# Another order for the single operations of attention and the first product group

## The chip, the cores and the metric

The kernel runs on one core of one Trainium2 chip. The metric is the device time of one execution in microseconds; lower is better. Within a core the engines work side by side, each through its own list of instructions in a fixed order: TensorE (PE) multiplies, VectorE (DVE), ScalarE (ACT) and GpSimd (POOL) do elementwise work, and SyncE (SP) issues the transfers between HBM and the on-chip memory (SBUF). An instruction waits on semaphores for its inputs and for the place it writes to, and whatever stands behind it on the same engine waits with it.

## The reference, cut to what matters

```python
# q, k, v: (4 batches, 8 heads, 576 tokens, 64); attention inside chunks of 64 tokens
scores = scale * np.matmul(q_c, k_c.transpose(0, 1, 2, 4, 3))
scores = scores - np.max(scores, axis=-1, keepdims=True)
attn = np.exp(scores)
attn = attn / (np.sum(attn, axis=-1, keepdims=True) + 1e-09)
out = np.matmul(attn, v_c)
x = out as 2304 tokens x 512
x = (x @ w_a) * (x @ w_b) @ w_out          # w_a, w_b 512 x 1536, w_out 1536 x 512
h = x @ w_in                               # 512 x 2048
g = np.maximum(h, 0.0) + alpha * np.minimum(h, 0.0)
return g @ w_out2                          # 2048 x 512
```

## The kernel before

The 2304 tokens are 18 units of 128, handled in nine pairs (0 to 8). The first pair makes up token block 0, pairs 1 and 2 block 1, 3 and 4 block 2, 5 and 6 block 3, 7 and 8 block 4. For attention each unit loads its q and k (512 KB, three buffers) and its v (three small transfers). The weights of the first product group come in blocks of 512 KB as 64-bit words, through two buffers, and are put together as float32 by ScalarE, VectorE and GpSimd; each is then split into a high and a low half. Every matrix product is three products of halves, 12 matmuls for a tile of 128 rows and one block of tokens.

The program has two parts. From the second on (`after_attention`) a planner orders everything by costs and due times. The first part, attention and the first product group on blocks 0 to 3, follows the string `START` near the top of the file: 304 words, each one operation, performed in that order (`perform`). So `START` sets the order on every engine, and it also sets who gets the next buffer of a ring: there are four PSUM banks for products and transposes, two PSUM places for scores and attention outputs (tag `s`), three SBUF places shared by the transposed probabilities and the first product of a group (tag `a`), two for probabilities (tag `e`).

A word is letters and a number: a pair, a pair's unit behind `U` (pairs 0 and 1 are done by unit), or block and part behind a dot. `t` and `c` count units throughout, so `t10` is the first unit of pair 5. The chain of one pair is

- `Lk` load q and k (SP, L1691), `s` scores (PE, L1735), `m` maximum (DVE, L1741), `u` subtract it (DVE, L1745), `e` exponential (ACT, L1751), `z` sum and `r` reciprocal (DVE, L1755, L1759 and L1760), `n` normalise (POOL, L1764)
- `t` transpose (PE, L1771), `c` copy out (ACT, L1778), `Lw` load v (SP), `v` times v (PE, L1793), `h` high half of x (ACT, L1812), `l` low half of x (DVE, L1816)

and that of one weight block is `Lf` load (SP, L248), `o` (ACT, L258 and L259), `d` (DVE, L266, L267, L270), `a` (POOL, L280), `H` high half (ACT, L285), `V` or `W` low half (POOL or DVE, L290). `F` is one product of the first layer (`F1.3`: block 1, part 3; even parts are a, odd parts b), `E` takes it out of PSUM (ACT L395 for even parts, DVE L405 for odd ones, which multiplies b by a), `h1.1` and `g1.1` are the halves of that result (ACT L376, POOL L381), `B` one product of the second layer and `D` its way out (ACT L432). Waits that matter below: `u` of a pair writes where the pair two before it had its probabilities, so it comes after that pair's `t`; a score tile goes where an older score tile or attention output was read last; a transfer waits until the transfer eight before it has landed.

The function `keep_busy` puts 24 matmuls on zeros among the first scores (L1685), behind the words `sU0`, `sU2` and `t0`; it is in both versions.

Of the kernel before, what the change touches and what calls it, by code (L numbers as in the profile page):

```python
# [27 lines left out]


START = """  # L30
Lk0 Lf0 sU0 Lk1 mU0 uU0 o0 d0 Lk2 sU1 mU1 eU0 zU0 rU0 sU2 Lf1 o1 uU1 a0 nU0 Lk3 mU2 sU3 Lk4 d1 Lk5 a1 Lw0
Lf2 uU2 Lw1 eU1 mU3 uU3 H0 eU3 zU1 t0 s2 V0 eU2 Lk6 Lk7 rU1 nU1 c0 o2 zU3 t1 c1 H1 vU0 zU2 rU2 Lw2 vU1 nU2
hU0 rU3 m2 hU1 Lw3 t2 nU3 t3 c3 Lk8 c2 u2 lU0 s3 lU1 e2 F0.0 E0.0 vU2 V1 vU3 d2 z2 Lw4 a2 r2 H2 F0.1 Lf3 n2
o3 m3 t5 hU2 u3 E0.1 V2 hU3 Lk9 Lw5 d3 Lk10 s4 lU2 lU3 a3 Lk11 Lw6 e3 t4 F0.2 Lk12 c5 c4 H3 m4 v2 u4 V3 F0.3
Lf4 h0.1 g0.1 z3 h2 l2 e4 E0.2 s5 r3 z4 F1.0 r4 Lf5 n3 o4 E0.3 E1.0 Lk13 t6 m5 d4 F1.1 h0.3 Lk14 t7 n4 c6
F1.2 E1.1 g0.3 o5 a4 u5 d5 a5 c7 e5 Lw7 t9 H4 z5 h1.1 g1.1 t8 v3 s6 H5 Lf6 F1.3 Lw8 h3 c9 r5 V4 E1.2 Lw9
Lk15 m6 V5 n5 c8 l3 B0.0 Lw10 u6 v4 E1.3 t11 t10 s7 o6 D0.0 m7 h1.3 h4 c11 l4 g1.3 d6 e6 B0.1 z6 B1.0 B1.1
c10 Lw11 a6 D0.1 D1.0 r6 Lf7 B0.2 o7 u7 v5 D0.2 h5 n6 D1.1 B1.2 Lw12 B0.3 d7 e7 Lk16 D0.3 B1.3 t12 D1.2 F2.2
D1.3 z7 Lw13 r7 n7 t13 c12 l5 F2.0 F2.3 Lw14 c13 v6 E2.2 E2.3 E2.0 t15 F2.1 t14 h6 l6 E2.1 F3.0 Lw15 Lk17
h2.3 h2.1 g2.3 c15 s8 Lw16 g2.1 B2.0 m8 H6 a7 c14 D2.0 E3.0 v7 F3.1 B2.1 E3.1 u8 F3.2 B2.2 h3.1 F3.3 h7 l7  # L40
Lf8 e8 z8 H7 Lf9 D2.1 r8 E3.2 Lw17 n8 D2.2 E3.3 g3.1 V6 t17 t16 B2.3 c16 c17 h3.3 g3.3 v8 h8 l8 D2.3 W7
"""


# [1861 lines left out]
```

## Time and profile before

| | us |
|---|---|
| median of 3 runs (lowest, highest) | 846.9 (846.26, 846.99) |
| the profiled execution, its own time | 845.54 |
| its span, first to last instruction | 843.6 |
| PE busy in the span | 833.2 |
| DVE, ACT, POOL busy | 704.3, 434.5, 199.3 |
| mean granted TensorE clock (share of full speed) | 0.998 |

The work of `START` ends on PE at about 100 us of the span. A busy PE counts matmuls that overlap, so the step from one start to the next is the better measure of what an operation takes.

### The profile page before, as it was taken

The page shows a single profiled execution, that of the slowest core. Times are in us where ns is not written, and L with a number is a line of the kernel's source. Part 1 is how long each engine was busy: PE and PEld are TensorE (multiplying, and loading weights), DVE is VectorE, ACT ScalarE, POOL GpSimd, SP SyncE. Part 2 cuts the span into 40 slices and gives each one's busy share as a digit, 9 for nine tenths or more (in the row PEclk, how much of TensorE's full clock was granted, in tenths as well). Part 3 has the DMA queues.
Part 4 walks back from the last instruction along what each step waited for, and adds up shares of the span by engine and source line. Part 5 has one row for each costly group of instructions (what it writes and reads, how often), then busy time and mean ns, then how long its engine had stood idle before and what let it go on. Part 6 is the DMA issues. An engine that isn't in the chain of part 4 may idle for free.

```text
span 843.6 us, 15744 instructions
## 1 busy us (share of the span) xinstructions
PE 833.2 (99%) x5676; PEld 727.8 (86%) x5676; DVE 704.3 (83%) x1165; ACT 434.5 (52%) x762; POOL 199.3 (24%) x158
## 2 busy tenths in 40 slices
PE   7999999999999999999999999999999999999998
PEld 6888888888888888888888888989999899999998
DVE  6983388988888989898899999999889876677786
ACT  4673576554555445554456567654336435444441
POOL 4553234423342321421321233111103000000000
PEclk9999999999999999999999999999999999999999
DMA  8953367778658531899999699897657679665543
GB/s 317 301 182 112 101 200 219 226 252 271 224 164 311 175 113 50 262 333 386 341 349 334 228 320 363 290 339 214 213 185 222 194 237 293 214 187 171 181 150 125
DMA packets 137357, 197.14 MB, mean 234 GB/s; under 512 B 15424, under 2 KB 79424, under 8 KB 137280
## 3 DMA queue, kind: packets, MB, share of 16 engines
q1 hardware_dynamic: 137280, 196.15, 70.2%
q8 instruction: 45, 0.74, 0.4%
q14 instruction: 32, 0.26, 0.1%
HBM read 138.42 MB, written 57.67 MB: 232 GB/s over the span
## 4 chain that ended last, share of the span: by engine, by line
PE 97%; DMA 1%; DVE 1%; ACT 0%; issue 0%; SPq 0%; DVEq 0%
PE po L368 20%; PE pa L368 11%; PE pb L368 11%; PE l4X L1444 11%; PE sumX L1042 10%; PE pX L1042 6%; PE l4Z L1444 5%; PE sumZ L1042 5%; PE pZ L1042 3%; PE l4Y L1444 3%; PE ph L368 3%; PE sumY L1042 3%; PE pY L1042 2%; PE s L1793 1%; PE pt L1771 1%; PE s L1735 1%
## 5 line engine op out<-in xcount | busy, mean ns | idle before, releaser
L728 POOL TENSOR_TENSOR t<-t,raw 128x512 int32<-128x512 int32 x60 | 82.8, 1380 | 249.7 <-DVE t L720 119.9
L1171 DVE TENSOR_TENSOR acc<-po,acc 128x512 f32<-128x512 f32 (+1 forms) x100 | 63.0, 633 | 15.5 <-PE po L368 14.6
L1042 PE MATMUL sumX<-T,w 128*128 128x512 f32 x248 | 65.6, 392 | 0.0
L368 PE MATMUL po<-gh,wl 128*128 128x512 f32 (+1 forms) x176 | 64.0, 364 | 0.0
L368 PE MATMUL po<-gl,wh 128*128 128x512 f32 (+1 forms) x176 | 63.6, 361 | 0.0
L368 PE MATMUL po<-gh,wh 128*128 128x512 f32 (+1 forms) x176 | 63.4, 360 | 0.0
L1444 PE MATMUL l4X<-w,h 128*128 128x256 f32 x308 | 62.7, 283 | 0.0
L368 PE MATMUL pa<-xh,wl 128*128 128x512 f32 (+1 forms) x160 | 58.0, 363 | 0.4 <-DVE wl L757 0.4
L368 PE MATMUL pb<-xh,wl 128*128 128x512 f32 (+1 forms) x160 | 57.8, 362 | 0.0
L368 PE MATMUL pa<-xl,wh 128*128 128x512 f32 (+1 forms) x160 | 57.3, 358 | 0.0
L368 PE MATMUL pb<-xl,wh 128*128 128x512 f32 (+1 forms) x160 | 57.3, 358 | 0.0
L368 PE MATMUL pa<-xh,wh 128*128 128x512 f32 (+1 forms) x160 | 57.2, 358 | 0.0
L368 PE MATMUL pb<-xh,wh 128*128 128x512 f32 (+1 forms) x160 | 57.2, 357 | 0.0
L753 ACT ACTIVATE wh<-t 128x512 fp32r<-128x512 f32 x60 | 37.6, 627 | 30.9 <-POOL t L728 29.0
L1042 PEld LDWEIGHTS sumX<-T,w 128*128 128x128 f32 x248 | 44.7, 189 | 7.7
L1444 PEld LDWEIGHTS l4X<-w,h 128*128 128x128 f32 x308 | 49.4, 191 | 1.2
L697 ACT ACTIVATE t<-raw 128x512 f32<-128x512 f32 x60 | 39.8, 664 | 15.4 <-DMA raw<-in_moe_w_out 7.7
L757 DVE TENSOR_TENSOR wl<-t,wh 128x512 fp32r<-128x512 f32 x52 | 42.4, 821 | 2.1 <-ACT wh L753 2.1
L1444 PE MATMUL l4X<-w,l 128*128 128x256 f32 x156 | 44.0, 282 | 0.0
L720 DVE SCALAR_TENSOR_TENSOR t<-raw,t 128x512 uint32<-128x512 uint32 x60 | 42.2, 704 | 1.3
L368 PE MATMUL po<-gh,w 128*128 128x512 f32 x128 | 43.2, 389 | 0.0
L702 ACT ACTIVATE raw<-raw 128x512 int32<-128x512 uint32 x60 | 40.0, 667 | 2.1 <-DMA raw<-in_moe_w_out 2.1
(272 smaller groups left out, 2419.2 us busy)
## 6 DMA issues: line engine op xcount, KB each, us to landing
w<-dw SPq DMA_DIRECT2D x134, 256.0 KB, 4.1
w<-dw SPq DMA_DIRECT2D x194, 128.0 KB, 3.3
dw<-wl SPq DMA_DIRECT2D x62, 256.0 KB, 4.5
dw<-wh SPq DMA_DIRECT2D x61, 256.0 KB, 4.9
raw<-in_moe_w_out SPq DMA_DIRECT2D x28, 512.0 KB, 4.2
qk_t<-in_qkv SPq DMA_DIRECT2D x18, 512.0 KB, 5.3
raw<-in_moe_w_in SPq DMA_DIRECT2D x16, 512.0 KB, 4.5
raw<-in_moe_w_a SPq DMA_DIRECT2D x12, 512.0 KB, 4.1
```

The source lines that it names most:

```text
L368: nc.tensor.matmul(out=dst, lhsT=a, rhs=b, start=(i == 0), stop=(i == len(steps) - 1))
L697: nc.scalar.activation(out=x, in_=st["raw"][:, :, 1].bitcast(F32), func=ACTF.Abs)
L702: nc.scalar.activation(out=lo.bitcast(I32), in_=lo, func=ACTF.Copy, scale=2.0**-29)
L720: nc.vector.scalar_tensor_tensor(out=u, in0=st["raw"][:, :, 1], scalar=0xC0000000, in1=u, op0=ALU.bitwise_and, op1=ALU.bitwise_or,)
L728: nc.gpsimd.tensor_tensor(out=i, in0=i, in1=st["raw"][:, :, 0].bitcast(I32), op=ALU.add)
L753: nc.scalar.activation(out=st["h"], in_=F[key], func=ACTF.Copy)
L757: ENG[t.engine].tensor_tensor(out=l, in0=F[key], in1=st["h"].bitcast(F32), op=ALU.subtract)
L1042: nc.tensor.matmul(out=dst, lhsT=x, rhs=y, start=opens and kk == n == 0, stop=kk == 1 and n == 2, skip_group_check=not opens,)
L1171: nc.vector.tensor_tensor(out=a, in0=b, in1=a, op=ALU.add)
L1444: nc.tensor.matmul(out=dst[:, tt], lhsT=x, rhs=y, start=opens and tt == i == 0, stop=i == 5, skip_group_check=tt > 0 or not opens,)
L1735: nc.tensor.matmul(out=s[q, i, kk, hp % 2, hp // 2 ^ i, :], lhsT=t[r, 0, hp, q], rhs=t[r, 1, hp, q])
L1771: nc.tensor.transpose(out=pt[:, h, i, :], in_=e[:, i, u % U, h].rearrange("p o k -> p (o k)"), identity=ident)
```

## The change

The 304 words of `START` are put in another order; the words are the same, no other line changes, and every operation still comes after what it needs. A line of it:

```diff
 START = """
-Lk0 Lf0 sU0 Lk1 mU0 uU0 o0 d0 Lk2 sU1 mU1 eU0 zU0 rU0 sU2 Lf1 o1 uU1 a0 nU0 Lk3 mU2 sU3 Lk4 d1 Lk5 a1 Lw0
+Lk0 Lf0 Lk1 sU0 Lk2 Lf1 mU0 o0 uU0 eU0 d0 zU0 sU1 Lk3 mU1 rU0 sU2 Lk4 Lk5 uU1 a0 mU2 o1 d1 sU3 eU1 zU1 nU0
...
```

The second part of the program is the same instruction for instruction. On PE the order is the same up to `F0.1`; after it attention runs further ahead (`t4` before `s4`, pairs 3 to 8 earlier), and all eight products `B1` and `B2` stand at the end of the part. On SP `Lf2` stands behind `Lw1 Lw0 Lk6`, where it stood behind `Lw0` alone, and `Lk9 Lw5` stand ahead of `Lk8 Lw4`.

On VectorE, behind the conversion of the second weight block (rows L266 to L270), the unit chains of pairs 0 and 1 stood like this before (`mx`, `e` and `sm` with the numbers 207 and 239, 308 are pair 1; `e_139`, `sm_167` are the second unit of pair 0):

```order
L1745 TENSOR_TENSOR e_239<-s_171,mx_207 128x2x256
L1741 TENSOR_REDUCE mx_207<-s_171 128x2x4
L1745 TENSOR_TENSOR e_239<-s_171,mx_207 128x2x256
L1755 TENSOR_REDUCE sm_167<-e_139 128x2x4
L1759 TENSOR_SCALAR sm_167<-sm_167 128x2x4
L1760 RECIPROCAL sm_167<-sm_167 128x2x4
```

And now (`e_146`, `sm_152` are pair 0, `e_234`, `sm_294` pair 1):

```order
L1755 TENSOR_REDUCE sm_152<-e_146 128x2x4
L1745 TENSOR_TENSOR e_234<-s_175,mx_207 128x2x256
L1759 TENSOR_SCALAR sm_152<-sm_152 128x2x4
L1760 RECIPROCAL sm_152<-sm_152 128x2x4
L1741 TENSOR_REDUCE mx_207<-s_175 128x2x4
L1755 TENSOR_REDUCE sm_294<-e_234 128x2x4
L1759 TENSOR_SCALAR sm_294<-sm_294 128x2x4
L1760 RECIPROCAL sm_294<-sm_294 128x2x4
L1745 TENSOR_TENSOR e_234<-s_175,mx_207 128x2x256
```

The sum and reciprocal of pair 0's second unit (`zU1 rU1`) stand ahead of the last maximum and subtraction of pair 1 (`mU3 uU3`), not behind them.

On ScalarE, from the second transposed unit (`c1`, `ptt_t_315`) to the third and fourth, before:

```order
L258 ACTIVATE t_305<-raw_237 128x512
L259 ACTIVATE raw_237<-raw_237 128x512
L1778 ACTIVATE ptt_t_315<-pt_310 128x512
L285 ACTIVATE wh_317<-t_199 128x512
L1812 ACTIVATE xh0_360<-s_319 128x4x128 x2
L1778 ACTIVATE ptt_t_383<-pt_378 128x512
L1778 ACTIVATE ptt_t_387<-pt_372 128x512
L1751 ACTIVATE e_389<-e_389 128x1024
```

And now (`c1` is `ptt_t_327`):

```order
L1778 ACTIVATE ptt_t_327<-pt_304 128x512
L285 ACTIVATE wh_353<-t_209 128x512
L1812 ACTIVATE xh0_355<-s_309 128x4x128 x2
L258 ACTIVATE t_362<-raw_329 128x512
L259 ACTIVATE raw_329<-raw_329 128x512
L1778 ACTIVATE ptt_t_370<-pt_365 128x512
L1751 ACTIVATE e_381<-e_381 128x1024
L1778 ACTIVATE ptt_t_436<-pt_376 128x512
```

The third weight block (`o2`, L258 and L259) went from ahead of `c1` to ahead of `c2`.

Later, on GpSimd, the stretch that ends in the normalising of pair 5 (`n5`, the last L1764 row) was this before (`a4 a5 g1.1 V4 V5 n5`):

```order
L280 TENSOR_TENSOR t_726<-t_726,raw_658 128x512
L280 TENSOR_TENSOR t_785<-t_785,raw_723 128x512
L381 TENSOR_TENSOR gl_813<-a_sb_730,gh_811 128x512
L290 TENSOR_TENSOR wl_914<-t_726,wh_807 128x512
L290 TENSOR_TENSOR wl_926<-t_785,wh_886 128x512
L1764 TENSOR_TENSOR e_789<-e_789,sm_809 128x1024
```

And it is now (`a4 a5 V4 g0.3 g1.1 V5 n5`):

```order
L280 TENSOR_TENSOR t_721<-t_721,raw_632 128x512
L280 TENSOR_TENSOR t_839<-t_839,raw_802 128x512
L290 TENSOR_TENSOR wl_914<-t_721,wh_904 128x512
L381 TENSOR_TENSOR gl_916<-a_sb_704,gh_899 128x256
L381 TENSOR_TENSOR gl_961<-a_sb_837,gh_912 128x512
L290 TENSOR_TENSOR wl_965<-t_839,wh_906 128x512
L1764 TENSOR_TENSOR e_730<-e_730,sm_866 128x1024
```

`g0.3` (256 columns) moved in between `a5` and `n5`. What `a5` (the second row) waits for is `d5` on VectorE, which now stands behind the taking out of `F0.3` and `F1.1`:

```order
L405 TENSOR_TENSOR a_sb_704<-pb_789,a_sb_704 128x256
L405 TENSOR_TENSOR a_sb_837<-pb_708,a_sb_837 128x512
L266 TENSOR_SCALAR t_839<-t_839 128x512
L267 TENSOR_SCALAR t_839<-t_839 128x512
L270 SCALAR_TENSOR_TENSOR t_839<-raw_802,t_839 128x512
```

Before, `F0.3` was taken out well ahead of it (`E0.3 m5 d4 E1.1 u5 d5`), since on PE `F0.3` came before `F1.0`; now `F0.3` comes after `F1.1 F1.0 v3`, and PE goes on with `s6 t8 t9 F1.3 F1.2 v4 s7 t10 t11 F2.0`.

## Rows read from the trace of the kernel before

**Rows 1.** The page: busy time, share and count by engine
```profile
PE 833.2 (99%) x5676; PEld 727.8 (86%) x5676; DVE 704.3 (83%) x1165; ACT 434.5 (52%) x762; POOL 199.3 (24%) x158
```

**Rows 2.** Stretches: start:end, length, busy by engine (count), PEclk, DMA share, GB/s
```profile
90.00:100.00 10.00, 10.00 (x106) 8.26 (x107) 4.13 (x6) 5.75 (x10) 4.86 (x4) 1.00 0.19 50
...
19.00:19.50 0.50, 0.49 (x18) 0.49 (x21) 0.41 (x1) 0.47 (x1) 0.50 (x1) 0.50 0.98 391
```

**Rows 3.** Waits of PE, 0 to 160: total us, times, longest
```profile
PE pt L1771 <- POOL e L1764: 1.8, 2, 1.5
```

**Rows 4.** Timeline of PE: start, us, instruction, idle time before and releaser
```profile
15.03 0.69 PE L1735 MATMUL s<-qk_t 64*64 64x64 f32 x32 [0.81 <-DMA qk_t<-in_qkv]
17.19 0.66 PE L1771 MATMUL pt<-ident,e 128*128 128x128 f32 x4 [1.46 <-POOL e L1764]
...
20.07 1.97 PE L1771 MATMUL pt<-ident,e 128*128 128x128 f32 x8
...
23.20 0.39 PE L368 MATMUL pa<-xh,wl 128*128 128x256 f32 x1
...
27.99 0.66 PE L1771 MATMUL pt<-ident,e 128*128 128x128 f32 x4 [0.37 <-POOL e L1764]
```

**Rows 5.** Timeline of DVE, pair 1's subtraction and pair 0's sum
```profile
12.97 0.68 DVE L1745 TENSOR_TENSOR e<-s,mx 128x512 f32<-128x512 f32 x1
14.89 0.68 DVE L1755 TENSOR_REDUCE sm<-e 128x8 f32<-128x512 f32 x1
```

**Rows 6.** Timeline of POOL, normalising pair 0's second unit
```profile
16.09 1.04 POOL L1764 TENSOR_TENSOR e<-e,sm 128x512 f32<-128x512 f32 x1 [0.39 <-DVE sm L1760]
```

**Rows 7.** Timeline of SP and ACT: Lf2 issued, Lk6 and Lk7 issued, o2
```profile
11.56 0.59 SPq L248 DMA_DIRECT2D raw<-in_moe_w_a  x1
...
15.06 0.82 SPq L1691 DMA_DIRECT2D qk_t<-in_qkv  x2
...
17.22 0.68 ACT L258 ACTIVATE t<-raw 128x512 f32<-128x512 f32 x1 [0.58 <-DMA raw<-in_moe_w_a]
```

**Rows 8.** Tile qk_t, 0 to 40: its loads
```profile
DMA to landing us min/median/max: 3.7/5.4/6.6
```

**Rows 9.** Timeline of PE later: a first-layer product, then v4, t11 and t10
```profile
36.91 0.50 PE L368 MATMUL pa<-xh,wl 128*128 128x512 f32 x1
...
39.77 0.60 PE L1771 MATMUL pt<-ident,e 128*128 128x128 f32 x4
...
52.84 1.16 PE L1793 MATMUL s<-ptt_t,v_t 64*64 64x64 f32 x64
53.93 1.09 PE L1771 MATMUL pt<-ident,e 128*128 128x128 f32 x8
```

**Rows 10.** Timeline of DVE later: d4's first step, E1.1, d5's first step, l3
```profile
40.65 1.03 DVE L266 TENSOR_SCALAR t<-t 128x512 f32<-128x512 f32 x1
...
43.25 0.69 DVE L405 TENSOR_TENSOR a_sb<-pb,a_sb 128x512 f32<-128x512 f32 x1
...
44.99 0.42 DVE L266 TENSOR_SCALAR t<-t 128x512 f32<-128x512 f32 x1
...
50.47 1.21 DVE L1816 TENSOR_TENSOR xl<-s,xh 128x1024 fp32r<-128x1024 f32 x1
```

**Rows 11.** Timeline of POOL later: a5, V4 and V5, n5
```profile
46.73 1.30 POOL L280 TENSOR_TENSOR t<-t,raw 128x512 int32<-128x512 int32 x1 [2.04 <-ACT e L1751]
...
49.23 2.56 POOL L290 TENSOR_TENSOR wl<-t,wh 128x512 fp32r<-128x512 f32 x2
51.73 1.92 POOL L1764 TENSOR_TENSOR e<-e,sm 128x1024 f32<-128x1024 f32 x1
```

**Rows 12.** Line 381 (g), 0 to 110: duration ns min/median/max, first and last start
```profile
L381 POOL TENSOR_TENSOR gl<-a_sb,gh x8: 741/1282/1306, 34.1 to 99.5; 128x512 fp32r<-128x512 f32 x6, 128x256 fp32r<-128x256 f32 x2
```

**Rows 13.** Timeline of ACT: an exponential, a copy of a transposed unit
```profile
45.11 1.06 ACT L1751 ACTIVATE e<-e 128x1024 f32<-128x1024 f32 x1 [0.83 <-DVE e L1745]
...
49.51 0.59 ACT L1778 ACTIVATE ptt_t<-pt 128x512 f32<-128x512 f32 x1
```

More of the change, by code (lines that the diff above doesn't have):

```diff
@@ L30 @@
 START = """
-Lk0 Lf0 sU0 Lk1 mU0 uU0 o0 d0 Lk2 sU1 mU1 eU0 zU0 rU0 sU2 Lf1 o1 uU1 a0 nU0 Lk3 mU2 sU3 Lk4 d1 Lk5 a1 Lw0
[L32 to L41, printed above, removed]
+Lk0 Lf0 Lk1 sU0 Lk2 Lf1 mU0 o0 uU0 eU0 d0 zU0 sU1 Lk3 mU1 rU0 sU2 Lk4 Lk5 uU1 a0 mU2 o1 d1 sU3 eU1 zU1 nU0
+uU2 t0 a1 eU2 rU1 Lw1 Lw0 mU3 c0 s2 H0 zU2 Lk6 nU1 rU2 uU3 m2 t1 vU0 eU3 c1 Lf2 V0 nU2 zU3 vU1 rU3 H1 hU0 hU1
+Lk7 nU3 o2 t2 c2 Lw2 t3 u2 lU1 lU0 Lw3 s3 e2 F0.0 c3 Lk9 d2 vU2 vU3 z2 r2 Lw5 Lk8 Lw4 V1 a2 m3 hU2 n2 hU3 H2
+u3 F0.1 t5 t4 Lf3 V2 e3 Lk10 c4 s4 E0.0 lU3 c5 Lk11 lU2 z3 r3 v2 h2 F0.2 o3 E0.1 Lf4 Lw6 m4 n3 h0.1 u4 t6 t7
+Lw7 c6 s5 g0.1 e4 l2 d3 a3 m5 E0.2 c7 F1.1 o4 H3 Lk13 V3 u5 Lk12 Lw9 F1.0 z4 e5 r4 v3 F0.3 Lf5 s6 E1.0 o5 n4
+d4 E0.3 E1.1 d5 Lk14 a4 t8 t9 m6 z5 h3 F1.3 F1.2 u6 h0.3 Lk15 a5 H4 H5 Lw8 h1.1 V4 g0.3 c8 l3 c9 Lw10 v4 e6
+g1.1 E1.2 V5 r5 s7 E1.3 n5 z6 h4 Lf6 t10 Lk16 t11 l4 o6 d6 c10 F2.0 h1.3 r6 m7 B0.1 B0.0 g1.3 Lk17 c11 s8
+Lw11 n6 Lw12 E2.0 Lf7 u7 D0.0 a6 v5 o7 B0.3 m8 D0.1 t12 Lw13 e7 t13 F2.1 h5 D0.3 u8 c13 z7 c12 r7 n7 B0.2 Lf8
+e8 D0.2 Lw14 v6 d7 E2.1 F2.2 h6 h2.1 g2.1 t14 t15 c15 l5 H6 Lw15 l6 E2.2 F2.3 z8 c14 r8 v7 Lw16 h7 F3.0 n8 V6
+t16 a7 l7 c16 E2.3 Lw17 t17 F3.2 h2.3 g2.3 E3.0 c17 v8 F3.1 E3.2 h8 E3.1 F3.3 Lf9 B1.3 B1.0 H7 D1.0 l8 W7
+D1.3 B1.2 E3.3 D1.2 B1.1 h3.1 h3.3 B2.0 B2.2 g3.1 D2.0 g3.3 B2.3 D1.1 B2.1 D2.2 D2.3 D2.1
 """
```

## The prediction, written before the changed kernel ran

> **What bounds the kernel now.** First the busy times: PE is at work for 833.2 of the span's 843.6 us [rows 1], so whatever leaves its matmuls as they are can win back ten microseconds at most. Then the stretches and the waits tell where the rest lies: at 90 to 100 PE is busy without a gap [rows 2], and between 0 and 160 it waits only in the first 36 us, longest for the normalising on POOL, 1.8 us in two waits [rows 3]. On the timeline of that stretch these are t1 at 17.19, 1.46 us late, and t5 at 27.99, 0.37 late; a q and k load costs 0.81 us ahead of 15.03 [rows 4]. From 19.0 the granted clock is 0.50 [rows 2], which is the 1.2 GHz level, and t2 and t3 take 1.97 us at it [rows 4], where a pair of transposes later takes 1.09 [rows 9]. So the change can win only ahead of about 36, and can lose anywhere up to 100, where the reordered part ends; after that the instructions are the same and PE-bound, so I carry a shift of that end through to the last instruction unchanged.
>
> **The first pairs: 1.3 us won.** Neither side of the table adds an instruction, so each step is a new waiting time. On DVE zU1 now stands where uU2 stood, at 12.97, and not at 14.89 [rows 5]. From zU1 to the normalising nU1 the trace has 16.09 - 14.89 = 1.20 us [rows 5, 6]; one subtraction of 0.68 now lies between, so nU1 starts at 12.97 + 1.20 + 0.6 = 14.8 and ends 1.04 later, 15.85. t1 comes at 15.9, straight behind the scores that start at 15.03, and not at 17.19.
> Not all of it stays. vU0 writes over pair 1's scores, which uU3 now reads last: behind zU1, rU1, mU3, zU2 and rU2 that is four steps of 0.65 and two short pairs of 0.4 from 12.97 on, so uU3 ends at about 16.95 and vU0 starts at 17.0. eU3, c1 (0.6 each) bring vU1 to 18.2. nU3 waits for zU3 and rU3, which now stand behind the 1.2 us maximum of pair 2, and ends near 20.15; t3 runs at 20.2, s3 at 20.8, and F0.0 at 21.9 instead of 23.20 [rows 4]: 1.3 us.
> I take the clock as full here. In the trace it fell after a stretch from 14 with waits of 0.81, 1.46 and 0.5 us; the new ones are 0.5, 0.5 and 0.8. If it falls all the same, the transposes and F0.0 lose the 0.9 us per pair that 1.97 against 1.09 shows, but t5, which the next step sets, hides 0.4 or more of that; the sum then goes up by 0.5 at most, and by 0.9 if nothing hides it.
> The Trainium skill ("TensorE: Matmul & The Clock Gate", Part 1) says that the clock halves once the array has been idle and comes back after sustained work, and names pauses longer than any in these rows as the ones to avoid. By that rule these pauses would not lower it at all; the row at 19.0 disagrees, and I leave the 0.5 as a bound.
>
> **The step to F1.1: 1.5 us won in all.** o2 now follows hU1 on ACT, at 20.0, with c2, e2 and c3 queued behind it. Its weights are issued later: Lf2 stands behind Lk6 and waits for Lk5's landing at 15.03, so about 15.05 instead of 11.56; Lf2 landed 5.66 us after its issue, just ahead of o2 at 17.22 [rows 7]. With 5.0 us the block is there when ACT is, with 5.66 ACT waits 0.7. I take 0. Then e2 runs to 22.75, z2 and r2 to 24.5, n2 (1.92, [rows 11]) to 26.5, and t5 starts at 26.55 instead of 27.99: 1.4 us.
> Scores s4 then need Lk8, which now stands behind Lk9 and Lw5. Lw5 waits for Lk7, issued at 15.5 as before [rows 7] and landed after 5.4, at 20.9 [rows 8]; its three issues bring Lk8 to 22.7, landed at 28.1 to 28.3. s4 could have run at 27.6, so 0.6 is lost again. Lk11 waits for the first half of s4, 28.8, and lands at 34.2; s5 ends at 34.75 and F1.1 starts. Before, F1.0 started at 36.91 [rows 9]; the new order has done t6 and t7 by then (1.0) and not F0.3 (1.6), so the equal place is 36.3. Won: 1.55 us. This term hangs on three landings in a row (Lk7, Lk8, Lk11): at the shortest, 3.7 [rows 8], they hide behind the work and F1.1 starts at 33.7, 2.6 won; at the longest, 6.6, it starts near 38.1, 1.8 lost. I take the median, 5.4.
>
> **The step to F2.0: 1.0 us lost.** Take T as the end of F0.3. From here PE sets the clock of everything: s6 1.09, t8 and t9 1.09, F1.3 and F1.2 two times 39.77 - 36.91 = 2.86, v4 and s7 1.09 each (52.84 to 53.93) [rows 9] put t10 at T + 10.1 if nothing is late.
> t10 needs n5. On DVE E0.3 (256 columns, 0.4; E1.1 with 512 is 0.69) and E1.1 now stand ahead of d5, and from d5's start to a5's the trace has 46.73 - 44.99 = 1.74 [rows 10, 11]. So a5 starts at T + 0.2 + 0.4 + 0.69 + 1.74, less 0.2 of overlap: T + 2.85. On POOL follow a5 1.30, V4 1.25 (two in 51.73 - 49.23), g0.3 0.74, g1.1 1.28, V5 1.25 and n5 1.92 [rows 11, 12]: n5 ends at T + 10.6, with the hand-over T + 10.75. PE waits 0.65 at t10, in a place where it had no wait before, t11 starting at 53.93 with n5 ending at 51.73 + 1.92 = 53.65 [rows 9, 11]. g0.3 is what turned the balance.
> F2.0 comes two transposes later, T + 11.85, and needs l4. c8 writes where g0.3 read, at T + 6.2; c8, c9 at 0.5 each (0.59 with overlap), e6 1.06 [rows 13], E1.2 0.6, then on DVE E1.3 0.69 [rows 10], z6 and l4 1.21 each [rows 10], less 0.1 of overlap a step: T + 12.2. Another 0.35 us; together 1.0.
> Bounds: a chain that overlaps as far as its rows allow leaves 0.5. If d5's first two steps ran beside POOL work, they would take what d4's did, 1.03 for the one that takes 0.42 in d5 [rows 10], and the wait would be 1.0 longer, 2.0; I expect them undisturbed, because POOL stands idle for them at that moment.
> The Trainium skill ("GPSIMD Engine Reference", Key points) says that GpSimd shares its SBUF interfaces with VectorE and that the two hinder each other in such modes. The pair 1.03 and 0.42 agrees; by the rule alone d5 stays at the lower figure here and the sum at 1.0.
>
> **The rest.** For v7, v8 and the late transposes I find every producer ahead of PE, v8 by as little as 0.1 us (c17); the eight products B at the end need only finished halves. I cost them at nothing, with 0.3 if c17 is late.
>
> **Sum.** -1.5 + 1.0 = -0.5 us. The profiled execution's own time, 845.54, becomes 845.0; it lies 1.36 below the median of the runs, 846.9, and on that scale the forecast is 846.4. What a measurement of this kernel can tell from no change is 0.2%, 1.7 us: 845.2 to 848.6.
>
> **Rivals.**
> *The loads in a row set the pace (slower).* Lk7, Lk8 and Lk11 each wait for the one before, directly or through s4. The stretch is one with a DMA share of 0.9 and more [rows 2], which speaks for landings above the median; that one weight block fewer stands ahead of them speaks against. At 6.0 each, three times 0.6 is lost: F1.1 at 36.55, no gain, and with the 1.0 of F2.0 the time is 846.9 + 0.25 + 1.0 = 848.2; beyond 6.15 it passes 848.6. It decides against the change from about 5.55 us each, where the gain is 1.0. Chance 0.20, half of it beyond 848.6.
> *The gain stands and the loss does not (faster).* Loads land in 4.5 to 5, F1.1 starts near 34, 2.3 won, and n5 and l4 come in time through overlap, 0.3 lost: 844.9. For it, the trace's POOL steps overlap a little; against it, the chain from F0.3 hangs on PE itself and no early gain loosens it. Chance 0.17.
> *Nothing changes where it counts.* The clock falls as before and o2 waits 0.7 for its block; t5 gains 0.7 only, and the end moves by 0 to +0.5: 847.2. Chance 0.13.
> *The forecast,* -1.6 to +0.9: 0.50.
>
> Faster by over 0.2% comes from the second rival (0.13 of it) and a tail of the forecast (0.04): 0.17. Slower comes from half of the first, 0.10, from parts of the third and from waits I have not found in 60 us of tight order, 0.08: 0.18. The range for eight in ten runs from the faster rival to just past the slower one, 844.9 to 848.7; the forecast's own is 845.3 to 847.8.
>
> **What would show it.** t1 near 15.9 and F0.0 near 22; a wait of s for a q and k load near 28 and another near 34; F1.1 before 36.3 less whatever is lost; after that no wait of PE until t10, there 0.5 to 1 us on POOL's L1764, then a short one of F2.0 on DVE's L1816; the end of the last product B at about 99.6. The prediction is wrong if PE waits elsewhere between 40 and 100, if the clock falls a second time, or if the second part, the same in both, starts to wait.

## The result: 5 us slower, and the profile after

| us | before | after |
|---|---|---|
| median (lowest to highest) | 846.62 (845.95 to 846.99, 6 runs) | 851.9 (850.22 to 853.23, 6 runs) |
| ratio, 95% interval | | 1.0062 [1.0049, 1.0075] |
| the profiled execution, its span | 845.54, 843.6 | 852.28, 850.2 |

The forecast was 846.4 with a range to 848.7: wrong, and in sign too. TensorE's first line of the page of the changed kernel [for rows 1], then four stretches (columns as in rows 2):

```profile
PE 835.3 (98%) x5676; PEld 729.7 (86%) x5676; DVE 706.0 (83%) x1165; ACT 435.6 (51%) x762; POOL 199.2 (23%) x158
```
```profile
19.00:19.50 0.50, 0.50 (x7) 0.36 (x4) 0.47 (x3) 0.42 (x1) 0.07 (x1) 1.00 0.55 190
30.00:35.00 5.00, 0.70 (x44) 0.56 (x36) 2.84 (x4) 0.00 (x0) 1.90 (x1) 0.88 1.01 356
35.00:40.00 5.00, 5.00 (x31) 4.55 (x35) 3.19 (x4) 3.31 (x6) 0.90 (x2) 0.50 0.62 200
90.00:100.00 10.00, 10.00 (x48) 8.28 (x45) 3.19 (x5) 2.85 (x6) 0.00 (x0) 1.00 0.43 159
```

The clock no longer falls at 19 [rows 2], but from 30 to 35 PE works 0.70 us of 5, ACT not at all, the DMA engines all the time, and the five after that are at 0.50. What PE waits for, 0 to 160 (total, times, longest):

```profile
PE s L1793 <- issue: 4.7, 2, 4.3
PE pt L1771 <- POOL e L1764: 2.1, 3, 0.9
PE s L1735 <- DMA qk_t<-in_qkv: 1.6, 4, 0.7
```

A wait of 4.3 us in the weighted sums (L1793) has "issue" as its cause, which is to say none that the profile shows. (The other of the two, 0.36, stands ahead of vU0 and comes back in most profiles of this order.) PE's timeline [for rows 4 and 9]:

```profile
16.21 0.65 PE L1771 MATMUL pt<-ident,e 128*128 128x128 f32 x4 [0.38 <-POOL e L1764]
...
20.53 0.66 PE L1771 MATMUL pt<-ident,e 128*128 128x128 f32 x4 [0.92 <-POOL e L1764]
...
22.00 0.69 PE L1735 MATMUL s<-qk_t 64*64 64x64 f32 x32 [0.19 <-DMA qk_t<-in_qkv]
22.63 0.39 PE L368 MATMUL pa<-xh,wl 128*128 128x256 f32 x1
...
27.09 1.09 PE L1771 MATMUL pt<-ident,e 128*128 128x128 f32 x8
28.46 1.16 PE L1735 MATMUL s<-qk_t 64*64 64x64 f32 x64 [0.28 <-DMA qk_t<-in_qkv]
29.42 1.17 PE L1793 MATMUL s<-ptt_t,v_t 64*64 64x64 f32 x57
34.89 0.49 PE L1793 MATMUL s<-ptt_t,v_t 64*64 64x64 f32 x7 [4.30 <-issue]
...
38.04 1.91 PE L1771 MATMUL pt<-ident,e 128*128 128x128 f32 x8
...
41.29 0.50 PE L368 MATMUL pb<-xh,wl 128*128 128x512 f32 x1
...
60.18 1.09 PE L1771 MATMUL pt<-ident,e 128*128 128x128 f32 x8 [0.84 <-POOL e L1764]
61.03 0.47 PE L368 MATMUL pa<-xh,wl 128*128 128x512 f32 x1
```

Down to v2 it is nearly the forecast: t1 16.21 (15.9), t3 20.53 (20.2), t5 27.09 (26.55), s4 28.46 (28.3), v2 29.42 (29.4, one score length behind s4). Then v2 stands still after 57 of its 64 matmuls, and what follows runs at half clock: the transposes t6 and t7 take 1.91, not the 1.09 of t10 and t11. F1.1 starts at 41.29, forecast 34.75. From there to 160 the only wait of PE that the kernel before did not have is the forecast one of t10, 0.84. The first matmul of the second part of the program, before and after:

```profile
100.16 0.50 PE L368 MATMUL po<-gh,wl 128*128 128x512 f32 x1
```
```profile
106.44 0.39 PE L368 MATMUL po<-gh,wl 128*128 128x512 f32 x1
```

That is 6.28 later, and the span ends 6.6 later: what lies behind is shifted nearly alike.

### The profile page after: what moved, and what is told of

It is laid out like the page before. It is cut to its first block, busy times and chain, and to the rows that moved or that the text cites. A ratio compares the mean times of both kernels' runs of the same rounds, so it can differ in the third digit from the quotient of the medians.

```text
span 850.2 us, 15748 instructions
## 1 busy us (share of the span) xinstructions
PE 835.3 (98%) x5676; PEld 729.7 (86%) x5676; DVE 706.0 (83%) x1165; ACT 435.6 (51%) x762; POOL 199.2 (23%) x158
## 4 chain that ended last, share of the span: by engine, by line
PE 92%; DMA 3%; DVE 3%; issue 1%; ACT 1%; POOL 0%; SPq 0%; DVEq 0%; ACTq 0%
PE po L368 19%; PE l4X L1444 10%; PE sumX L1042 10%; PE pa L368 10%; PE pb L368 10%; PE pX L1042 6%; PE l4Z L1444 5%; PE sumZ L1042 5%; PE pZ L1042 3%; PE l4Y L1444 3%; PE ph L368 3%; DMA qk_t<-in_qkv 3%; PE sumY L1042 3%; PE pY L1042 2%; PE s L1793 1%
## 5 line engine op out<-in xcount | busy, mean ns | idle before, releaser
L1171 DVE TENSOR_TENSOR acc<-po,acc 128x512 f32<-128x512 f32 (+1 forms) x100 | 63.0, 634 | 15.8 <-PE po L368 14.8
L706 DVE TENSOR_SCALAR t<-t 128x512 f32<-128x512 f32 x60 | 31.1, 519 | 18.9 <-ACT t L697 18.7
```

The costliest lines, as they stand in the source:

```text
L706: nc.vector.tensor_scalar(out=F[key], in0=F[key], scalar1=LOW64, scalar2=TOP64, op0=ALU.max, op1=ALU.min)
L1171: nc.vector.tensor_tensor(out=a, in0=b, in1=a, op=ALU.add)
```

## The experiments

Theory A: the place behind the 57th matmul is a place in PE's own program, and PE waits there for its next instructions. The page counts `q8 instruction: 45, 0.74` MB in both kernels, 16.4 KB a packet; PE's 5676 matmuls and 5676 weight loads in 45 packets make 126 matmul records a packet. The page counts the time of these packets against the same 16 DMA engines as the loads. Rival B: v2 waits for data. Rival C: the loss is the half clock alone. (A record is one matmul in the timeline; a border, the place where one packet's instructions end.) "Before" is the kernel before on the same chip; each profile is of one execution.

| run | median (lowest to highest, runs) | before | ratio [95%] |
|---|---|---|---|
| e1 F0.2 ahead of v2 | 850.53 (848.10 to 853.97, 7) | 846.44 | 1.0048 [1.0027, 1.0070] |
| e2 t0 fill 7 | 849.35 (847.18 to 852.41, 10) | 846.44 | 1.0036 [1.0019, 1.0052] |
| e3 loads after v2 | 856.58 (853.72 to 857.01, 4) | 846.44 | 1.0113 [1.0088, 1.0138] |
| e5 before, F0.2 behind v2 | 848.25 (846.50 to 850.93, 10) | 846.44 | 1.0020 [1.0006, 1.0035] |
| e9 after again | 849.96 (847.90 to 852.93, 6) | 846.12 | 1.0048 [1.0029, 1.0067] |
| e6 20 records more | 848.89 (847.35 to 852.78, 11) | 846.12 | 1.0039 [1.0025, 1.0053] |
| e7 the same, d5 first | 850.89 (850.15 to 852.20, 5) | 846.12 | 1.0057 [1.0043, 1.0071] |
| e4 d5 first | 854.18 (852.71 to 855.20, 4) | 846.12 | 1.0093 [1.0077, 1.0109] |
| e10 Lf2 early | 851.34 (850.08 to 851.77, 5) | 846.78 | 1.0053 [1.0041, 1.0065] |
| e11 before, Lf2 late | 849.19 (847.93 to 851.63, 7) | 846.78 | 1.0033 [1.0021, 1.0044] |
| e12 Lf2 early, 20 records | 850.12 (848.62 to 852.88, 6) | 846.78 | 1.0049 [1.0033, 1.0065] |
| e13 the same, n5 first | 849.99 (847.13 to 852.60, 9) | 846.78 | 1.0032 [1.0016, 1.0049] |
| e14 early part only | 847.14 (846.70 to 849.73, 12) | 846.36 | 1.0016 [1.0007, 1.0025] |
| e15 later part only | 850.10 (847.72 to 850.43, 5) | 846.36 | 1.0037 [1.0025, 1.0050] |
| e16 after, small loads | 848.16 (846.33 to 848.73, 11) | 846.36 | 1.0014 [1.0004, 1.0024] |
| e17 before, small loads | 845.53 (844.79 to 846.25, 11) | 846.36 | 0.9988 [0.9979, 0.9997] |
| e18 early part, loads as before | 846.47 (845.83 to 849.56, 12) | 846.42 | 1.0003 [0.9991, 1.0014] |
| e19 n5 first | 850.03 (848.19 to 852.14, 8) | 846.42 | 1.0039 [1.0023, 1.0054] |

### Is it a place in the program?

**e1.** In the changed order:

```diff
-v2 h2 F0.2 o3
+F0.2 v2 h2 o3
```


> The changed kernel with one word moved: F0.2 (12 matmuls, 1.63 us) stands ahead of v2 on PE, as it did before the change. Theory A, the 4.3 us in v2 are PE without instructions: its instruction stream comes in blocks of 16 KB through a DMA queue of its own, and the last seven matmuls of v2 are the first of a block that has not landed. Then PE has 1.65 us more to do ahead of the same place in its instructions, the stop moves 12 matmuls forward in v2 (after some 45 of its 64 records) and shrinks by about 1.6, to 2.7 us or less; the clock may still fall; about 850 us. Rival B, v2 waits for its data (the v transfers or the copied transposes): the stop stays after record 57 and v2 ends when it did, 35.4 us; 851.9. Rival C, the loss is the falling clock by itself and not the stop: the same time as the changed kernel.

PE in e1, v2:

```profile
33.96 0.92 PE L1793 MATMUL s<-ptt_t,v_t 64*64 64x64 f32 x44
36.36 0.56 PE L1793 MATMUL s<-ptt_t,v_t 64*64 64x64 f32 x20 [1.49 <-issue]
```

F0.2 has 12 records, and the stop came after 44 instead of 57. A second one, 1.05 us, stood in s3 after 28 records. Between the two lie 36 + 12 + 64 + 12 + 8 + 64 + 12 + 44 = 252 records (the rest of s3, F0.0, pair 1's sums, F0.1, t5 and t4, s4, F0.2, v2): two packets of 126.

**e5.** In the order of before:

```diff
-t4 F0.2 Lk12 ... v2 u4
+t4 Lk12 ... v2 F0.2 u4
```


> The kernel before with one word moved: F0.2 stands behind v2 on PE instead of ahead of it, the reverse of the first experiment. The kernel before has a stop of 0.39 us in v2 after 46 of its 64 records. Theory A: the stop moves to about record 58 of v2 and grows by about 1.6 to some 2.0 us, the clock may fall behind it; 848 to 850 us. Rival B: v2 has its data 1.6 us later than it is now wanted at worst; if the stop is data, it falls at a place where an instruction waits (its first, third, fourth, or the same of its second half). Rival C: no change, 846.6.

The timeline shows no stop, where about 2.0 us had been expected: v2 began only at 32.95, held 1.52 us by ScalarE's copies, and its next instructions came almost in time. In the single starts of the trace the 59th record of v2 comes 0.32 us behind the 58th, where 0.04 is usual: the place is the expected one, the length is not. The kernel lost 0.2%, within the range, but mostly through another wait. In the kernel before the stop had been in sight; I had passed over these rows:

```profile
32.33 0.92 PE L1793 MATMUL s<-ptt_t,v_t 64*64 64x64 f32 x46
33.64 0.56 PE L1793 MATMUL s<-ptt_t,v_t 64*64 64x64 f32 x18 [0.39 <-issue]
```

**e6.** The changed kernel, with a step that only adds records:

```diff
                 keep_busy(idle[token])
+            if token == "t0":
+                short(10)   # ten products of zero[0:64, 0:64] with itself
```


> The changed kernel with ten short products on zeros (64 rows x 64 columns, 20 matmul records, about 0.45 us) behind those that follow t0, where TensorE stands 0.75 us before the second half of s2 anyway. No other instruction moves. Theory A: every border between instruction blocks comes 20 records earlier in the program: the one in t5 moves into pair 1's weighted sums (crossed near 25.5 instead of 27.4, where the DMA share was 0.42 instead of about 1.0), the one in v2 from record 57 to about record 37. The block for it is then asked for about 2 us earlier and in a quieter stretch: the stop in v2 is gone or under 1 us, the clock holds to F1.1, which starts at 35 to 37 instead of 41.3, and the time is 845 to 848.5. Rival B (the stop belongs to v2, or to its loads): it stays at record 57 with 3 to 4 us, F1.1 near 41, and the time is 850.5 to 853.

No stop, full clock, F1.1 at 36.58, as expected; the median, 848.89, is just above the expected range. s3 waited 1.72 for Lk7 instead. **e12** adds to it Lf2 ahead of `Lw1 Lw0`, **e13** also n5 ahead of V5.

> Lf2 early as in the first of these runs, and the ten short products on zeros behind those of t0, which move every border between instruction blocks 20 matmul records ahead. Theories A and C together: no wait of s3 over 0.4, no stop in v2 over 0.5, F1.1 starts at 34.5 to 36, and what is left against the kernel before is the wait of t10 on POOL (0.8 to 1.5): 845.5 to 847.5. If either cause is something else, the time stays at the 848.9 that the short products alone gave, or above.

> The run before, and POOL does n5 ahead of V5 (its 1.3 us subtraction for the weights). Theory: t10, which waits for n5, starts up to 1 us earlier (its wait falls from 0.8 to 1.5 to at most 0.5), since V5's result is wanted only after v5; the time falls by 0.4 to 1 against the run before, to 844.8 to 846.8, level with the kernel before or ahead of it. Rival: V5, now later, is waited for itself (by F2.1 or a product behind it) and nothing is won.

e12: no stop, but waits for loads in s3 (0.89), s4 (0.73) and s5 (1.58): in s3 under 0.4 was expected, and the median, 850.12, missed its range too. PE in e13, v2 and the second matmul of F2.0:

```profile
29.70 0.79 PE L1797 MATMUL s<-ptt_t,v_t 64*64 64x64 f32 x37
33.76 1.12 PE L1797 MATMUL s<-ptt_t,v_t 64*64 64x64 f32 x27 [3.28 <-issue]
...
60.53 0.50 PE L368 MATMUL pa<-xl,wh 128*128 128x512 f32 x1 [0.58 <-DVE xl L1820]
```

The stop is back, after 37 records: 57 less the 20 added. That settles the place, and with it A against B. C is out as well: in the first profile PE stood still for 4.30 us, whatever its clock. But the stop of e13 is 3.28 long, so coming to the border earlier did not cure it. The n5 exchange took t10's wait away, and VectorE's remainder (l4) for F2.0 took 0.58 in its place: nothing won, against 0.4 to 1 expected.

### Why so long, and not always?

**e9.** The changed kernel, nothing edited.

> The changed kernel once more, nothing edited. Theory A (TensorE waits for its own next block of instructions, which comes by the same DMA engines as the loads): the stop in v2 comes again after the same number of records of v2 (55 to 59 of 64), because it is a place in the program and not in time, but its length is another one, anywhere from 0 to 5 us, since the block's packet queues behind whatever loads are in flight; the time is 850 to 853. From the packet on queue 8 to the first matmul behind the stop it is again about 2.3 us. Rival B (v2 waits for data that the trace does not name, such as values or copies): the stop sits elsewhere in v2, or is just as long (4.3) wherever it sits.

```profile
23.36 1.14 PE L1735 MATMUL s<-qk_t 64*64 64x64 f32 x32 [1.57 <-DMA qk_t<-in_qkv]
...
31.48 1.65 PE L1793 MATMUL s<-ptt_t,v_t 64*64 64x64 f32 x64
...
36.93 0.50 PE L368 MATMUL pb<-xh,wl 128*128 128x512 f32 x1
...
55.98 1.09 PE L1771 MATMUL pt<-ident,e 128*128 128x128 f32 x8 [0.96 <-POOL e L1764]
...
102.06 0.39 PE L368 MATMUL po<-gh,wl 128*128 128x512 f32 x1
```

In this execution (847.90) the timeline shows no stop in v2. Its 64 records take 1.65 us, though, where 1.16 is usual, and in the single starts of the trace the 58th comes 0.31 us behind the 57th: the stop is there, in its place, and 0.3 long. From v2 to F1.1 took 5.45 us, forecast 5.35, and in the first profile 11.87, which is 6.42 more, the stop and the half clock behind it. Up to v2 it is the other way round: e9 is 2.06 behind there, since its s3 waited 1.57 for Lk7 and the clock was at 0.50 from 23.0 to 26.3. The difference, 4.36, is that of their F1.1, and the two executions of one program differ by 4.38. The packet tells when the instructions came. DMA queues in two stretches of the first profile of the changed kernel, from the border in t5 on (queue, kind: packets, MB, share of 16 engines):

```profile
q1 hardware_dynamic: 1078, 1.67, 103.6%
```
```profile
q1 hardware_dynamic: 96, 0.36, 91.5%
q8 instruction: 1, 0.02, 5.8%
```

From 27.3 to 32.5 there are 1078 packets of loads and none of instructions; the one from 32.5 to 33.5 starts at 32.57, and v2 goes on at 34.89. In e9 PE is at the same border at 29.6, the loads take less of the DMA engines, and the packet comes 0.8 us later (30.3 to 31.3):

```profile
q1 hardware_dynamic: 136, 0.13, 61.9%
q8 instruction: 1, 0.02, 6.0%
```

The same for other stops (those of e1 and e4, and the short ones in s3 of e10 and e15, are alike):

| stop | PE at the border ahead | packet starts | PE goes on | from packet |
|---|---|---|---|---|
| after, v2 | 27.3 | 32.57 | 34.89 | 2.3 |
| e10, v2 | 27.3 | 31.52 | 33.82 | 2.3 |
| e15, v2 | 27.4 | 31.38 | 33.60 | 2.2 |
| e13, v2 | 25.6 | 31.52 | 33.76 | 2.2 |
| e16, v2 | 26.7 | 29.62 | 31.87 | 2.3 |
| before, v2 | 28.2 | 31.24 | 33.64 | 2.4 |
| e19, s3 | 15.3 | 21.7 | 24.42 | 2.7 |
| e3, s3 | 15.7 | 21.88 | 24.48 | 2.6 |
| e14, s3 | 15.5 | 20.57 | 23.08 | 2.5 |

From packet to matmul it is always 2.2 to 2.7, and this holds for the shorter stops too. Counted one by one in the trace, PE's matmuls, weight loads and semaphore instructions are 11,555, which makes 257 in each of the 45 packets. The stops stand at PE's 706th instruction (in s3) and its 1218th (in v2, once the 1217th), 512 apart, with a border in t5 halfway, in either order and whatever was moved. The 20 profiles have 60 passages of these three borders. At 17 of them the next matmul starts over 0.2 us behind the last one, always 2.2 to 2.7 us after the packet's start, the 0.3 of e5 and e9 among them. At the other 43 PE came 2.4 to 8.1 us after that start and ran through. So what PE waits for is the packet.

What varies is how long the packet comes after PE has passed the border ahead of its own: -0.1 to 6.4 us over the 60 passages of three borders (those that lie in s2, s3 and t5 of the changed order), 2.3 on the average, the same border in the same program 5.3 once and 0.8 once. The DMA share is a weak guide to it: in the three passages with a share under 0.5 in the 2 us to either side the packet came 1.2 late at most, in the others 2.4 on the average, from 0.2. That the loads make it late is not shown by this.

The Trainium skill ("Runtime: NRT & Kernel Launch", Instruction fetch mechanics) says that instructions come in 16 KiB blocks of 256 over a DMA queue that the sequencer drives, and that a border's cost is mostly hidden. The 45 packets of 16.4 KB agree; "mostly hidden" holds in the first profile from about 120 on, where the packets start 16 us and more apart and PE has no wait on "issue", and not at 4.3 us in v2.

**e3.** Quiet the loads around v2 (order of SP):

```diff
-Lw4 Lf3 Lk10 Lk11 (v2) Lf4 Lw6 Lw7
+Lw4 Lw6 (v2) Lw7 Lk10 Lk11 Lf3 Lf4
```


> The changed kernel with its transfers in another order on SP only: Lw6 comes right after Lw4, and Lw7, Lk10, Lk11, Lf3 and Lf4 follow v2. Lw7 waits for v2's first half, so nothing is issued from about 28 until 30 and the data queue is empty when PE's next instruction block is fetched. Theory A with its second half, that the block's transfer was late because it stood behind data: the stop in v2 shrinks from 4.3 to under 1.5 us. Lk10 and Lk11 are then issued at about 31 to 32 and land near 36 to 37, so PE waits for s5 instead, 2 to 3 us; the time 849 to 852. Theory A without that half, the fetch takes a fixed time from where PE crossed the last border: the stop stays at 4 us and s5 waits little; 852 to 854. Rival B: v2 waits as before, 4.3.

No stop on "issue" in v2 (the packet came 0.2 us after the passage at a share of 0.47), which agrees with a packet that is late for the loads, but it is one case. 2.38 stood on "issue" in s3, before the edit takes effect, and 3.24 in s5 for the late Lk10 and Lk11: 856.58, above the expected 849 to 852. That is what those loads are early for.

**e16 and e17.** Smaller loads in both orders (the scores from the fourth load on use a quarter of q for all heads and for k):

```diff
-nc.sync.dma_start(out=t..., in_=qkv[u, :, 0:2 * HP * P])
+nc.sync.dma_start(out=t[:, 0, 0:2]..., in_=qkv[u, :, 0:2 * P])   # u >= 3
```


> The changed kernel, but from the fourth load on a load of queries and keys brings 128 KB instead of 512 (one quarter of the tile; the scores then use that quarter for all heads, so part of the computation is replaced, with the same instructions on every engine). Theory A with the loads: with the DMA engines less busy the instruction block for v2 comes in time and s3 waits for nothing: no stop in v2 over 0.5, no wait of s3 over 0.4, F1.1 starts at 34.5 to 36, and the time is 844 to 847, spread over less than 2 us. Rival B (the loss is in the order itself, whatever the loads): 850 or more.

> The kernel before with the same small loads. Theory A with the loads: it loses its own waits for loads (1.7 us in its profile) and the stop of 0.4 in v2, and comes to 843.5 to 846.5; the changed kernel with small loads is then within 1 us of it on either side, where with full loads it was 4 to 5 us behind. Rival B: the changed kernel is still 3 us or more behind.

From 15 to 35 the DMA share falls from 0.93 to 0.67 in the changed order and from 0.89 to 0.55 in the other. The changed order loses no more for Lk7, but stops in v2:

```profile
28.49 1.28 PE L1798 MATMUL s<-ptt_t,v_t 64*64 64x64 f32 x57
31.87 0.49 PE L1798 MATMUL s<-ptt_t,v_t 64*64 64x64 f32 x7 [2.10 <-issue]
```

848.16 against 845.53: 2.6 behind, where with full loads it was 3.8 to 5.3. I had expected under 1 (A with the loads as cause) or over 3 (B), and missed both. What the smaller loads won need not be the stop: s3's wait for Lk7 is gone too, which was 1.57 in e9, and a stop of 2.10 lies between the 0.3 and the 4.30 that full loads gave. So that the loads make the stop longer is not shown here; the DMA engines were still two thirds busy.

**e2.** Longer filling, `t0=3` to `t0=7`:

> The changed kernel with four matmuls on zeros more behind t0 (seven instead of three), where PE waits anyway for a q and k load; 8 matmul records and 8 weight loads more in PE's stream, nothing else. Theory A: the same block border falls 8 matmul records earlier in the work, so the stop comes after about record 49 of v2 instead of 57, some 0.15 us earlier, and is about as long, 4.3 to 4.5 us; time as the changed kernel, 851.9 within 1.5. Rival B (data): the stop stays after record 57. Rival C says nothing on the place.

No stop in v2, where one after record 49 was expected: 1.98 in s3 for Lk7, then half clock, another wait in its place. **e10** puts Lf2 ahead of `Lw1 Lw0`, **e11** does the reverse in the kernel before (`Lk6 Lf2 Lk7`).

> The changed kernel with one load moved: Lf2 (512 KB) goes out right after Lk5 again, ahead of Lw1, as in the kernel before, where the change has it between Lk6 and Lk7. Theory C (TensorE, earlier at every step up to s3, runs into the loads, and Lk7 lands late because Lf2's 512 KB are in flight beside it): the second half of s3, which waited 0.2 us for Lk7 in the first profile of the changed kernel and 1.6 to 2.2 in most of the others of this order, waits under 0.4. Theory A alone then has TensorE early at the border in v2, so the stop there is the long one (1 to 4.5 us); together they give 848.5 to 851.5. Rival (Lf2 has nothing to do with it): s3 waits 1 to 2 as often as before, and the time is that of the changed kernel, 850 to 852.

> The kernel before with the same load moved the other way: Lf2 between Lk6 and Lk7, as in the changed kernel, nothing else. Theory C: s3, which in the kernel before waits for nothing of note, now waits 0.5 to 1.5 us for Lk7, the later loads of queries and keys follow, and the time rises by 0.7 to 2, to 846.8 to 848.2. Rival: no more than 0.4 from the kernel before.

e10: s3 waits 0.40, on "issue" and not for Lk7, and v2 stops for 3.44: as expected, 851.34. e11 was 2.4 slower, but through another mechanism, 3.43 us of PE for ScalarE's copy (in that order the copy stands behind o2, which needs Lf2). It says nothing on Lk7, and with e12's 0.89 the theory that Lf2 alone delays Lk7 (theory C in the texts of e10 to e12) is not shown.

### Which part of the change costs what?

**e14** takes the changed order up to `t3` and the order of before behind it, **e15** the reverse.

```diff
+START = first part of after (to t3), then the rest of before in its order   # e14
+START = first part of before (to t3), then the rest of after in its order   # e15
```


> The order of the changed kernel for everything up to t3 (pair 0, pair 1's first steps, their loads), and the order of the kernel before for all that follows. Theory A with the loads (TensorE comes earlier to loads and instruction blocks that come no earlier): t1 near 16.2 and s3 near 21.1 as in the changed kernel, but then a wait in s3 or at the next border takes the gain back, and the time is 846 to 849. The prediction on record had 1.3 us won here and kept: 845.2. Rival B (all of the loss sits in the later part): 845 to 846.

> The other half: the order of the kernel before up to t3, the order of the changed kernel after it. Theory A: TensorE comes to t5 about 1 us later than in the changed kernel, so the stop in v2 is shorter on the average; the wait at t10 on POOL (0.8 to 1.5) stays: 847 to 850. Rival (the early part is what costs): 846 to 847.

The early part costs 0.8, the later 3.7; together 4.5, where the whole costs 3.8 to 5.3. In e14's profile s3 starts at 20.60, where before it did at 21.97, and then PE stands at the border in it:

```profile
23.08 0.80 PE L1735 MATMUL s<-qk_t 64*64 64x64 f32 x36 [1.80 <-issue]
```

e15 stops in v2 after 57 records for 3.05 and waits 0.83 at t10.

**e18** is e14 with SP's order of before (`Lw0 Lf2 Lw1 Lk6 Lk7`).

> The order of the changed kernel up to t3 on TensorE, VectorE, ScalarE and GpSimd, the order of the kernel before for all later steps and for every load (Lf2 ahead of Lw1 again). The early part alone, with its own order of loads, had 847.1. If the early gain of about 1 us is kept where neither a load nor the next instruction block is late, the time is 844.8 to 845.8, ahead of both kernels. Theory A expects that mostly it is not kept: TensorE comes earlier to s3 and to the border in it, and stands there for what it gained or more: 846 to 847.5.

846.47, the kernel before again. Its profile reaches s4 at 27.67 and then waits 1.43 for the load of s4's second half: what was gained early is given back. No version here that does the whole computation beats the kernel before.

**e4, e7, e19** go after t10: d5 ahead of E0.3 (`o5 E1.0 ... d5 a5 E0.3`), in e7 with the 20 records, and n5 ahead of V5.

> The changed kernel with o5 ahead of E1.0 and d5 with a5 ahead of E0.3 (their order of before), and nothing else. Both theories leave the stop in v2 where it was, with another length. If the wait at t10 is a term of its own, it goes from 0.84 (1.3 to 1.5 in three variants) to under 0.3 and the median falls by 0.5 to 1.0, to 851.0 to 851.5; if it is covered by what follows (F2.0 and v5 have their own partners), the median stays at 851.9 within 0.4.

> The short products of the run before, and besides o5 and d5 in their order of before: o5 ahead of E1.0 and d5 with a5 ahead of E0.3, so that POOL has the chain to n5 earlier. Theory A, with the wait at t10 as the second term: the wait of t10 on POOL (0.84 in the changed kernel, 1.3 to 1.5 in three variants) goes to under 0.3 and the program ends 0.5 to 1 earlier than with the short products alone: 844.5 to 847.5. Rival B for this part (the wait at t10 only moves to the next thing that waits, F2.0 on ScalarE's l4 or v5): no more than 0.3 from the run before.

> The changed kernel with one exchange on GpSimd: n5 ahead of V5. t10's wait on n5 (0.84 in the changed kernel's first profile, 0.7 to 1.6 in the others of its order) goes to under 0.2; the stop in v2 and the waits of s3 stay as they are. If the wait at t10 is a term of its own, what TensorE loses between s7 and B0.0 falls by 0.4 to 1 us, and the median of the changed kernel (849.96 to 851.9) by as much as far as its spread lets it be seen: 849 to 851. If V5 or the remainder for v5 on VectorE takes its place, nothing is won.

All three missed. With d5 first t10's wait fell only to 0.70, and t9 now waits for VectorE, which does E0.3 later. From e4:

```profile
50.98 0.65 PE L1771 MATMUL pt<-ident,e 128*128 128x128 f32 x4 [0.88 <-DVE a_sb L405]
...
59.84 1.09 PE L1771 MATMUL pt<-ident,e 128*128 128x128 f32 x8 [0.70 <-POOL e L1764]
```

In e7 t9 waits 1.62. In e19 n5 came no earlier (t10 waits 0.88), as r5 ahead of it was late, and 0.59 came on top in F2.0, for l4. In these three orders each step forward on VectorE or GpSimd made another late.

## Why the prediction was wrong

**The first pairs (-1.3): the mechanism right, the size half.** zU1 and nU1:

```profile
13.20 0.68 DVE L1755 TENSOR_REDUCE sm<-e 128x8 f32<-128x512 f32 x1
```
```profile
15.12 1.04 POOL L1764 TENSOR_TENSOR e<-e,sm 128x512 f32<-128x512 f32 x1 [0.41 <-DVE sm L1760]
```

forecast 12.97 and 14.8 [rows 5, 6]; t1 0.3 late on the sum. F0.0 came at 22.63, not 21.9: 0.6 won. Of the rest, 0.3 is t3's lateness and 0.4 went in s3, whose second half waited for Lk7 till 22.00, and in e9 till 23.36. The sum had weighed Lk7 only as the load ahead of Lk8; that s3, now 0.9 earlier, could catch up with it, was not asked. The full clock at 19 came as assumed, against the fall in before [rows 2]; in e9 it fell at 23, in the wait of s3, and F0.0 took 2.48 instead of 1.62.

**The step to F1.1 (-1.5): the step that failed.** Its first half held. ScalarE's timeline has o2 at 20.43 (20.0), 0.26 late for its block (0 taken, 0.7 allowed for):

```profile
20.43 0.70 ACT L258 ACTIVATE t<-raw 128x512 f32<-128x512 f32 x1 [0.26 <-DMA raw<-in_moe_w_a]
```

With before's v2 at 32.33, less F0.2's 1.65, v2 is 1.26 ahead of the equal place, 30.68. From there before took 5.62 to the place equal to F1.1 (36.3), the forecast had 5.35, and it took 11.87 (5.45 in e9). The term left out PE's own instructions: the new order puts t5, t4, s4 and v2 back to back, 129 records up to the stop in 3.4 us, where before F0.2's long products stood between. The stop took 4.30, the half clock some 2 (11.87 - 5.45 - 4.30). Against the 0.39 of before, 1.65 of the stop is F0.2 gone from ahead of v2, and 2.2 is the packet, which started 5.3 after the border ahead was passed and 3.0 in before: the first is the order's, the second differs from run to run. The bounds (2.6 won to 1.8 lost, or 2.05 lost if three landings of 6.6 are each counted in full) were drawn from the landings of loads alone and could not hold it.

**The step to F2.0 (+1.0): right.** V5 and n5:

```profile
56.98 1.28 POOL L290 TENSOR_TENSOR wl<-t,wh 128x512 fp32r<-128x512 f32 x1
58.22 1.91 POOL L1764 TENSOR_TENSOR e<-e,sm 128x1024 f32<-128x1024 f32 x1
```

t10 waited 0.84 (0.65), in the other profiles that keep this part of the order 0.8 to 1.6. F2.0's 0.35 on l4 did not show at 61.03; its terms add up to T + 11.97 before any overlap is taken off, not to T + 12.2, so that 0.1 at most was due. From F1.1 to the second part it took 106.44 - 41.29 = 65.15, in e9 102.06 - 36.93 = 65.13, before 100.16 - 36.3 = 63.86: 1.3 lost, 1.0 forecast.

**The rest (0): right** up to 106; no new wait there.

**The rivals.** The nearest was the loads in a row, 848.2: it had TensorE meet the DMA engines, and put the wait at s4 and s5. s4 waited 0.28, s5 nothing of note in this profile, and the loads of q and k were not slower [for rows 8]:

```profile
DMA to landing us min/median/max: 3.7/5.1/6.8
```

Transfers decided, as that rival had it, but those of PE's own instructions. "The clock falls a second time" was named as what would make the forecast wrong; it fell at 33.8, while PE stood in the stop.

**The account of the profiled execution:** v2 1.26 earlier; 11.87 instead of 5.62 from there to F1.1, 6.25, of it 4.30 the stop and about 2 the half clock; 1.29 from F1.1 on: -1.26 + 6.25 + 1.29 = 6.28, which is 106.44 - 100.16. Without a long stop the forecast was still not met. In e9 (847.90) v2 is 0.80 later than the equal place, by s3's wait of 1.57 and the half clock behind it; from there to F1.1 0.17 was won, and 1.27 lost from F1.1 on: 1.90, which is 102.06 - 100.16. In e6 (847.91) s3 waited 1.72, s5 0.47 and 0.42, t10 1.41. So of the 1.5 that the forecast had won up to F1.1 nothing was kept in any of these profiles.

**Open:** what sets how late an instruction packet starts; that it is the loads in flight is argued, by 1078 packets of loads ahead of the late one and by e3, and not shown. In e13 and e6 the same border in t5's place was passed at 25.6 and 26.4, and the packet came 5.9 and 1.6 later. Nor was a kernel run with the transfers of that stretch fully away.

## What to carry to other kernels

A wait marked "issue" in the middle of a run of equal matmuls, at the same record count from run to run, was here the engine's own program arriving. Count records from there to the next such place, and allow for it before packing short matmuls together: what PE did from the border in t5 to the one in v2 took 5.0 us in the kernel before (28.2 to 33.2) and 3.3 in the new order (27.3 to 30.6), and the packet did not come sooner for it. A step that makes an engine earlier is worth what the next thing it needs allows, so follow the gain through every load and every block to the one that comes no earlier. And when one program's own runs differ by 5 us, profile it twice before explaining one profile.

## What the runs showed of the hardware

- A block of about 126 matmuls with their weight loads is ready for TensorE 2.2 to 2.7 us after its packet starts (17 stops, 20 profiles), and in the first 40 us the packet started up to 6.4 us after TensorE had passed the border ahead.
- With small loads the kernel before gained 0.1% though its timeline had 1.7 us of waits for them: in e17 t1 waited 2.56 for GpSimd, 1.46 before.
- The changed order spreads over 847.90 to 853.23 in its 12 runs; the kernel before over 845.19 to 849.86 in all of these comparisons, with medians of 846.1 to 846.8.
